# Another seven-product form for probabilities times values in a Conformer block, with four sums a pair, one convolution tap on ScalarE, and five orders moved

## The chip, the cores and the metric

The kernel runs on one core of one Trainium2 chip. A core has TensorE (PE, with a separate row PEld for its weight loads), VectorE (DVE), ScalarE (ACT), GpSimd (POOL) and SyncE (SP); each takes its instructions strictly in the order in which the program issues them, and waits at the head of its queue where an operand is not ready. SP issues nearly all DMAs, so they start in its order too. The metric is the time of one execution on the device in microseconds (us).

## The reference, cut to what matters

One Conformer block in bfloat16, with two sequences of 4000 tokens, D = 512 and F = 2048:

```python
h = _layernorm(x);  x1 = x + 0.5 * (_silu(h @ w_ff1_a) @ w_ff1_b)
h = _layernorm(x1)
p = softmax((h @ w_q) @ (h @ w_k).T * D**-0.5)          # per sequence, 4000 x 4000
x2 = x1 + (p @ (h @ w_v)) @ w_o
h = _layernorm(x2) @ w_pw1                               # 512 -> 1024
h = h[..., :D] * _sigmoid(h[..., D:])
dc = h[t-1] * dw[0] + h[t] * dw[1] + h[t+1] * dw[2]      # depthwise, 3 taps
dc = (dc - mean over all tokens) / sqrt(var + 1e-05)
x3 = x2 + _silu(dc) @ w_pw2
h = _layernorm(x3)
return _layernorm(x3 + 0.5 * (_silu(h @ w_ff2_a) @ w_ff2_b))
```

## The kernel before, in words

**Stages.** Tokens are cut into 16 chunks (eight a sequence) of 508, that is four tiles of 127; the last chunk of each sequence has 444. The stages follow one another: the first feed-forward layer (ff1), attention, and an end with the convolution, pw2 and the second feed-forward layer (ff2). Attention has 16 blocks g of queries, one per chunk, and each has 32 steps kt, one per tile of 128 keys. In the steady state a step is about 2 us and a block about 65.5 us.

**Folded weights.** Queries carry the product of w_q and w_k, so the keys are the normalised rows themselves, and w_v and w_o are folded into one matrix that is applied after the product with the values (`project`). Hence the "values" h[kt] are the normalised rows too: 128 keys by 512, and batch 1's replace batch 0's in block 8.

**Products by seven.** Scores of tile kt go to one of three PSUM banks (a ring, also used by the query groups, the convolution's pw1 and the projection), and ScalarE writes their exponentials to SBUF (`exp_pair`, all ScalarE work has line 710). Two key tiles make a pair; 15 pairs, one tile alone (`P30`) and a tail of 32 keys (`ptail`) make the 4000 keys. A pair by the two halves of the queries, and the 512 columns of the values by their two halves, is a product of 2 x 2 blocks, done with seven block products instead of eight. Each needs sums of probabilities (`pair_sums`, DVE, once a query block, line 1466, over a group of two pairs at a time) and sums of values (`v_sums`, line 1553, once a sequence; `v_here` for batch 0, `v_ahead` and `v_back` for batch 1, through DRAM buffers vhd and vfd). The seven products accumulate over all pairs in PSUM banks 3 to 7 (`PV_BANK`, `pv`, `pv_rest` for the lone tile and the tail), and `pv_join` (line 1527, and copies on ScalarE) combines the banks to the output. Since there are five banks for seven products, two products of a block are computed after others have been joined: `units` issues the work of a block step by step and `units_late` the rest of it in the first steps of the next block; `attention_end` does the latter for the last block. Row sums of probabilities accumulate in `acc` (lines 1472 and 1475), are split into two bfloat16 parts (`split_sums`, lines 1795 and 1796), turned to one column per query by SP's DMA transposes (`sums_by_query`; the issue shows as line 718), and divide the projected rows (`project`, `residual`, line 925).

**What else runs in attention.** `att_hook` adds, per step, the layernorm of the block's chunk before (`ln_job` at kt 9, its tiles' statistics and norms deferred by the numbers of its plan), the transposition of these norms by DMA (line 718, tile `work`), pw1 and the gate of the convolution (`conv_b`, `conv_a`, line 1887), and the three taps with their statistics (`taps_beside`, lines 1917, 1918, 1925, 1928) for chunks whose pw1 is done. `put_x` and `get_x` store and fetch the residual rows.

**What sets the order.** The order is written out by hand. Work that is not issued in place is deferred:

```python
def after(self, n, fn):
    self.later.append((self.tick_n + n, self.seq, fn))
```

and `tick()` at the end of each step issues what is due; `after(n)` called in step kt runs at the end of step kt + n - 1. Semaphore waits are emitted by `Sync.op` from the buffers that an instruction reads and writes. All matmuls have line 660.

**The lines of the change's other places.** ff1 ends with `late`, a table of plans for the layernorms of the last three chunks, which run in the first steps of attention. `keys_swap` places `v_here`, `v_ahead` and `v_back`; `tail_scores` computes the 32-key tail, adds it to the row sums (line 1754) and sends it through DRAM to `ptail`. `wa_back` (line 1073) loads 2 MB of summed ff2 weights (wsd) for ff2; it is issued in ff2's first chunk.

Of the kernel before, what the change touches and what calls it, by code (L numbers as in the profile page):

```python
# [259 lines left out]
class Conformer:  # L260
# [31 lines left out]
    def memory(self):  # L292
# [34 lines left out]
        self.Tt = [E.view(x, self.NTS * HC).rearrange("p (n k) -> p n k", k=HC) for x in (oTe, oTo)]  # L327
        self.b_T = [[E.buf("T", x + n * 2 * HC, 2 * HC) for n in range(self.NTS)] for x in (oTe, oTo)]
# [69 lines left out]
        homes = [(self.XR, 8192 + i * 1536) for i in range(10)] + [(C, oP + i * 1536) for i in range(PAIRS - 10)]  # L398
        self.VF = [Q.view(x, 3 * HD).rearrange("p (m d) -> p m d", m=3) for Q, x in homes]
        self.b_VF = [Q.buf("VF", x, 3 * HD * 2) for Q, x in homes]  # L400

        def both(i):
            Q, x = homes[i]
            n = min(2, PAIRS - i)
            return Q.view(x, n * 3 * HD).rearrange("p (n m d) -> p n m d", n=n, m=3)

        self.VF2 = [both(2 * j) for j in range(FC // 2)]
# [4 lines left out]
        self.vfd = nc.dram_tensor("vfd", [PAIRS, 128, 3 * HD], BF16, kind="Internal").ap()  # L412
        self.b_vhd = [Buf("vhd") for _ in range(PAIRS)]
        self.b_vfd = [[Buf("vfd") for _ in range(2)] for _ in range(PAIRS)]
# [1007 lines left out]
    def next_queries(self, g, kt, at):  # L1422
# [5 lines left out]
        if g + 1 < NCK and kt in ((3, 4, 14, 16) if g == 1 else (14, 16, 18, 20)):  # L1428
            self.q_group((g + 1) // TCB, (g + 1) % TCB, (3, 4, 14, 16).index(kt) if g == 1 else (kt - 14) // 2)
# [6 lines left out]
    def exp_pair(self, g, kt, ps, b_ps):  # L1436
# [5 lines left out]
        lo, hi = ((oR + n * 4 * HC, oTe + m * 2 * HC), (oTo + m * 2 * HC, oR + n * 4 * HC + 2 * HC))[odd]  # L1442
# [3 lines left out]
                 [self.b_R[n] if not odd else self.b_R2[n], self.b_T[odd][m]], scale=SCALE)  # L1446

    def pair_sums(self, g, j, step):
# [168 lines left out]
    def units_late(self, o, kt):  # L1617
# [20 lines left out]
        elif kt < 7:  # L1638
# [8 lines left out]
            if kt == 4:  # L1647
                self.pv_join(o, 5)
# [829 lines left out]
```

## Time and profile before

| | |
|---|---|
| median of 3 runs | 1917.2 us (1916.89 to 1919.14) |
| profiled execution | 1916.96 us, span 1912.9 us from first to last instruction |
| mean granted TensorE clock | 0.999 |
| ff1, 0 to 411 us | PE busy 408.43 us, DVE 336.98, ACT 289.52 |
| attention, 420 to 1435 us | PE 1010.47, DVE 757.25, ACT 431.75 |
| end with ff2, 1435 to 1912 us | PE 469.56, DVE 396.41, ACT 344.48 |

In the profile a group or an instruction is named by its line, its engine, its operation and `out<-in`, the tiles by the program's names: `sums` holds probabilities and their sums, `work`, `wff`, `xt` and `keys` are large regions used for several things, `s` and `y` are PSUM banks (0 to 3 and 4 to 7). SPq is SP's queue as it issues DMAs. A timeline line has the start in us, the length in us, the instruction, how many of a kind follow in one, and in brackets the idle time before it and what ended it. A line of the waits has the engine and tile, the line, the releaser, and then the idle time in all, the number of waits and the longest, in us.

### The profile page before, as it was taken

How to read it: one execution, taken by the hardware profiler on the slowest of the kernel's cores; microseconds unless marked ns; L12 is line 12 of the kernel's file. 1: busy time of each engine (PE TensorE's matmuls, PEld its weight loads, DVE VectorE, ACT ScalarE, POOL GpSimd, SP SyncE). 2: the span in 40 equal slices, each digit the busy share in tenths (PEclk: the TensorE clock that was granted, in tenths of full speed). 3: DMA queues.
4: the chain of work that ended last, by engine and by line, in shares of the span. 5: the costliest groups of instructions: out<-in, count | busy, mean ns of one | idle time of the engine just before them, and what ended most of it. 6: DMA issues, size and time to landing. Idle time of an engine off the chain costs nothing.

```text
span 1912.9 us, 35411 instructions
## 1 busy us (share of the span) xinstructions
PE 1896.8 (99%) x14186; PEld 1400.5 (73%) x14186; DVE 1496.7 (78%) x3220; ACT 1070.2 (56%) x1828; POOL 122.9 (6%) x235
## 2 busy tenths in 40 slices
PE   9999999999999999999999999999999999999998
PEld 6899999966666656666666566566665898999897
DVE  7788888767767787777777776767788888888885
ACT  5677777744443444344434434443447677777774
POOL 1000000000000000000000000000002000000000
PEclk9999999999999999999999999999999999999999
DMA  8233344293223332224821211221146222312211
GB/s 187 72 89 86 81 113 108 70 234 108 77 70 86 85 86 73 53 56 98 202 54 50 55 34 43 56 51 43 40 110 192 76 70 67 76 50 53 64 43 43
DMA packets 284731, 158.04 MB, mean 83 GB/s; under 512 B 204424, under 2 KB 271307, under 8 KB 284303
## 3 DMA queue, kind: packets, MB, share of 16 engines
q1 hardware_dynamic: 283881, 155.37, 32.3%
q8 instruction: 113, 1.85, 0.4%
q14 instruction: 59, 0.48, 0.1%
q10 hardware_dynamic: 678, 0.34, 0.1%
HBM read 62.24 MB, written 48.18 MB: 58 GB/s over the span
## 4 chain that ended last, share of the span: by engine, by line
PE 94%; DVE 3%; DMA 2%; ACT 1%; SPq 1%; issue 0%; POOL 0%; POOLq 0%; DVEq 0%; ACTq 0%
PE s L660 53%; PE y L660 40%; DMA work<-work 1%; DVE work L773 1%; ACT work L710 0%; DMA sums<-in_w_ff_a_dram 0%; DVE xt L925 0%; SPq L718 0%; DMA wff<-in_w_ff_a_dram 0%; DMA wff<-keysd 0%; DVE sums L1466 0%; DMA pqd<-wff 0%; DVE sums L1065 0%; SPq L722 0%; DVE work L958 0%
## 5 line engine op out<-in xcount | busy, mean ns | idle before, releaser
L710 ACT ACTIVATE sums<-s 128x508 bf16<-128x508 f32 (+2 forms) x608 | 355.9, 586 | 473.2 <-PE s L660 455.1
L660 PE MATMUL s<-work,keys 128*128 128x508 bf16 (+3 forms) x2240 | 505.5, 357 | 1.6 <-ACT sums L710 1.1
L660 PEld LDWEIGHTS s<-work,keys 128*128 128x128 bf16 (+1 forms) x2240 | 191.7, 97 | 159.9 <-issue 9.5
L710 ACT ACTIVATE keys<-s 128x508 bf16<-128x508 f32 (+1 forms) x281 | 163.8, 586 | 175.6 <-PE s L660 112.2
L1466 DVE TENSOR_TENSOR sums<-sums 128x508 bf16<-128x508 bf16 (+3 forms) x640 | 218.9, 396 | 35.8 <-ACT sums L710 32.8
L660 PE MATMUL y<-work,keys 128*127 128x256 bf16 x1920 | 244.7, 273 | 0.0
L660 PEld LDWEIGHTS y<-work,keys 128*127 128x127 bf16 x1920 | 216.3, 137 | 5.2
L660 PE MATMUL y<-wff,keys 128*127 128x256 bf16 (+3 forms) x1560 | 209.3, 277 | 0.6 <-DVE xt L1012 0.5
L773 DVE BATCH_NORM_STATS2 work<-xt 127x6 f32<-127x512 bf16 x311 | 199.3, 681 | 2.9 <-DMA xt<-in_x_dram 2.8
L660 PE MATMUL s<-sums 128*128 128x254 bf16 x1296 | 194.4, 273 | 1.6 <-DVE s L1121 1.6
L660 PE MATMUL s<-work,wff 128*128 128x508 bf16 (+4 forms) x884 | 185.5, 352 | 2.6 <-DMA work<-work 2.3
L660 PEld LDWEIGHTS y<-wff,keys 128*127 128x127 bf16 (+1 forms) x1560 | 175.8, 136 | 12.2 <-DVE xt L1012 1.6
L710 ACT ACTIVATE work<-xt,work 127x512 bf16<-127x512 bf16 x204 | 161.6, 808 | 16.9 <-DVE work L785 15.8
L971 DVE TENSOR_TENSOR keys<-keys 128x1016 bf16<-128x1016 bf16 x240 | 160.3, 680 | 2.8 <-ACT keys L710 0.7
L780 POOL TENSOR_TENSOR work<-work 127x4 f32<-127x4 f32 (+1 forms) x76 | 77.2, 1016 | 1153.8 <-DVE work L778 1153.8
L660 PE MATMUL s<-work 128*127 128x512 bf16 (+2 forms) x557 | 142.7, 381 | 1.3 <-DVE work L2091 1.2
L660 PEld LDWEIGHTS s<-sums 128*128 128x128 bf16 x1296 | 126.7, 98 | 19.9 <-DVE s L1121 1.9
L1475 DVE TENSOR_TENSOR work<-work,sums 128x508 f32<-128x508 f32 (+1 forms) x208 | 139.4, 670 | 1.1
L660 PE MATMUL y<-sums,xt 128*128 128x254 bf16 (+1 forms) x960 | 139.1, 269 | 0.8 <-DVE sums L1466 0.8
L660 PEld LDWEIGHTS s<-work,wff 128*128 128x128 bf16 x884 | 81.6, 98 | 75.5 <-issue 3.8
L660 PE MATMUL y<-work,wff 128*128 128x254 bf16 (+1 forms) x892 | 135.3, 274 | 0.0
L660 PEld LDWEIGHTS y<-sums,xt 128*128 128x128 bf16 x960 | 92.9, 97 | 57.6 <-DVE sums L1466 1.3
(151 smaller groups left out, 2510.6 us busy)
## 6 DMA issues: line engine op xcount, KB each, us to landing
xd<-xt SPq DMA_DIRECT2D x28, 448.0 KB, 2.8
xt<-xd SPq DMA_DIRECT2D x28, 448.0 KB, 3.5
out_dram<-xt SPq DMA_DIRECT2D x14, 448.0 KB, 3.2
dcvd<-wff SPq DMA_DIRECT2D x48, 127.0 KB, 2.0
keys<-dcvd SPq DMA_DIRECT2D x12, 508.0 KB, 4.7
xt<-in_x_dram SPq DMA_DIRECT2D x13, 448.0 KB, 4.4
wff<-in_w_ff_b_dram SPq DMA_DIRECT2D x8, 512.0 KB, 7.3
keys<-keysd SPq DMA_DIRECT2D x32, 128.0 KB, 2.9
```

The lines of the kernel that those rows point to most:

```text
L660: self.S.op("PE", lambda e: e.matmul(out, lhsT, rhs, start=start, stop=stop, **kw), reads=reads, writes=[bank], inc=stop if inc is None el ...
L710: return self.S.op("ACT", lambda e: e.activation(out, in_, func, **kw), reads=reads, writes=writes)
L773: self.S.op("DVE", lambda e: e.bn_stats(self.st[sl][:, ti, 0:6], x), reads=[b_x], writes=[self.b_st[sl][ti]])
L780: S.op("POOL", lambda e: e.tensor_tensor(out=self.rs[sl][:, 0:n], in0=self.mv[sl][:, 0:n, 1], in1=self.neghalf[0:TILE, 0:n], op=ALU.pow), ...
L971: self.S.op("DVE", lambda e, out=out, x=x, y=y, op=op: e.tensor_tensor(out=out, in0=x, in1=y, op=op), reads=rd, writes=wr)
L1466: S.op("DVE", lambda e: e.tensor_tensor(out=out, in0=x, in1=y, op=op), reads=rd, writes=wr)
L1475: S.op("DVE", lambda e: e.tensor_tensor(out=acc, in0=acc, in1=sig[step - 5], op=ALU.add), reads=b_f[0:2] + [self.b_acc[s]], writes=[self.b ...
```

## The change

Seven products stay, in another form. With a11, a21 the exponentials of the even key tile for the two query halves and a12, a22 those of the odd one, four sums are formed in a chain, s1 = a21 + a22, s2 = s1 - a11, s3 = a11 - a21 (in a21's place) and s4 = a12 - s2, where there were five. Each exponential instruction now writes both its halves into one kind of buffer. The row sums of the pairs accumulate (s4, s1), and since s4 + s1 = a11 + a12 one addition at the end of the block (the fold) makes them the sums of both halves. The tail is added to the row sums by one instruction over 32 partitions (`sum_tail`) from `ptail`, instead of four. Values' sums are four chained single-width subtractions, and lie in two buffers, V4 and V12; V4 has its own loads in block 8. The joins are two copies on ScalarE and five additions on DVE, instead of three and six. Product 1 now reads raw value tiles and is the first of a block, at step 7; the raw tiles were first read at step 9. The work left for the next block's first steps is in another order (`late_first`, `late_second`, `late_third`).

The multiplication of the first tap is done on ScalarE (Identity with a scale per partition) in place of DVE's tensor_scalar.

Five orders are moved: the layernorm of chunk 14 at the start of attention (plan 2,2,3,3,4,6,6,6,7,7 to 5,5,6,6,7,8,8,9,9,10); batch 0's sums of values (group 0 before attention, group j three steps earlier) and batch 1's (one step later); the layernorm before the convolution one tick earlier; block 1's query groups (3,4,14,16 to 3,4,12,14) and the last block's fetches (15,20,25 to 16,24,31); and the load of the summed ff2 weights, from ff2's first chunk to right behind `attention_end`.

The diff, cut to its core (buffers' declarations, the code of `v_sums` and the old body of `attention_end` are left out):

```diff
-        lo, hi = ((oR + n * 4 * HC, oTe + m * 2 * HC), (oTo + m * 2 * HC, oR + n * 4 * HC + 2 * HC))[odd]
+        lo, hi = ((oTo + m * 2 * HC, oTe + m * 2 * HC), (oR + n * 4 * HC, oR + n * 4 * HC + 2 * HC))[odd]
...
-        a11, a22 = R[:, :, 0], R[:, :, 1]
-        te, to = [t[:, m:m + n, 0:hw] for t in self.Tt]
-        b_te, b_to = [b[m:m + n] for b in self.b_T]
-        b_11, b_22 = self.b_R[r:r + n], self.b_R2[r:r + n]
-        f = [ft[:, k, 0:n, 0:hw] for k in range(3)]
-        if step < 5:
-            out, x, y, op, rd, wr = ((f[0], a11, to, ALU.add, b_11 + b_to, [b_f[0]]),
-                                     (f[1], te, a22, ALU.add, b_te + b_22, [b_f[1]]),
-                                     (f[2], a11, a22, ALU.add, b_11 + b_22, [b_f[2]]),
-                                     (te, te, a11, ALU.subtract, b_te + b_11, b_te),
-                                     (to, to, a22, ALU.subtract, b_to + b_22, b_to))[step]
+        a12, a22 = R[:, :, 0], R[:, :, 1]
+        a11, a21 = [t[:, m:m + n, 0:hw] for t in self.Tt]
+        b_11, b_21 = [b[m:m + n] for b in self.b_T]
+        b_12, b_22 = self.b_R[r:r + n], self.b_R2[r:r + n]
+        s4, s1, s2 = [ft[:, k, 0:n, 0:hw] for k in range(3)]
+        if step < 4:
+            out, x, y, op, rd, wr = ((s1, a21, a22, ALU.add, b_21 + b_22, [b_f[1]]),
+                                     (s2, s1, a11, ALU.subtract, b_11 + [b_f[1]], [b_f[2]]),
+                                     (a21, a11, a21, ALU.subtract, b_11 + b_21, b_21),
+                                     (s4, a12, s2, ALU.subtract, b_12 + [b_f[2]], [b_f[0]]))[step]
             S.op("DVE", lambda e: e.tensor_tensor(out=out, in0=x, in1=y, op=op), reads=rd, writes=wr)
             return
         acc = self.acc[s][:, 0:W].rearrange("p (h k) -> p h k", h=2)
+        if step == 6:
+            S.op("DVE", lambda e: e.tensor_tensor(out=acc[:, 0], in0=acc[:, 0], in1=acc[:, 1], op=ALU.add),
+                 reads=[self.b_acc[s]], writes=[self.b_acc[s]])
+            return
         sig = [ft[:, 0:2, k, 0:hw] for k in range(n)]
         if j == 0:
-            if step == 5:
+            if step == 4:
                 S.op("DVE", lambda e: e.tensor_tensor(out=acc, in0=sig[0], in1=sig[1], op=ALU.add),
                      reads=b_f[0:2], writes=[self.b_acc[s]])
-        elif step - 5 < n:
-            S.op("DVE", lambda e: e.tensor_tensor(out=acc, in0=acc, in1=sig[step - 5], op=ALU.add),
+        elif step - 4 < n:
+            S.op("DVE", lambda e: e.tensor_tensor(out=acc, in0=acc, in1=sig[step - 4], op=ALU.add),
                  reads=b_f[0:2] + [self.b_acc[s]], writes=[self.b_acc[s]])
 
-    PV_BANK = {1: 4, 6: 5, 7: 6, 5: 7, 3: 7, 2: 3, 4: 3}
+    PV_BANK = {1: 4, 6: 5, 7: 6, 5: 7, 3: 3, 2: 4, 4: 6}
 
...
-            form, b_1, mv, b_2 = {1: (v[:, 0], b_v, f[:, 2], b_f[2]), 2: (he[:, 0:HD], b_he, f[:, 1], b_f[1]),
-                                  3: (he[:, HD:D], b_he, R[:, 0], self.b_R[r]), 4: (ho[:, 0:HD], b_ho, R[:, 1], self.b_R2[r]),
-                                  5: (ho[:, HD:D], b_ho, f[:, 0], b_f[0]), 6: (v[:, 1], b_v, T[0], self.b_T[0][m]),
-                                  7: (v[:, 2], b_v, T[1], self.b_T[1][m])}[n]
+            he, ho, v4, v12 = self.h[2 * i], self.h[2 * i + 1], self.V4[i // 2][:, i % 2], self.V12[i // 2][:, i % 2]
+            b_he, b_ho, b_v4, b_v12 = self.b_h[2 * i], self.b_h[2 * i + 1], self.b_V4[i], self.b_V12[i]
+            form, b_1, mv, b_2 = {1: (he[:, 0:HD], b_he, T[0], self.b_T[0][m]), 2: (ho[:, 0:HD], b_ho, R[:, 0], self.b_R[r]),
+                                  3: (ho[:, HD:D], b_ho, f[:, 0], b_f[0]), 4: (v4[:, 0], b_v4, R[:, 1], self.b_R2[r]),
+                                  5: (v12[:, 0], b_v12, f[:, 1], b_f[1]), 6: (v12[:, 1], b_v12, f[:, 2], b_f[2]),
+                                  7: (he[:, HD:D], b_he, T[1], self.b_T[1][m])}[n]
...
-        forms = {5: (v[:, HD:D], b_v, 0), 2: (v[:, 0:HD], b_v, 1), 7: (vs, b_vs, 0), 6: (vs, b_vs, 1)}
+        forms = {3: (v[:, HD:D], b_v, 0), 7: (v[:, HD:D], b_v, 1), 2: (v[:, 0:HD], b_v, 0), 4: (vs, b_vs, 1)}
...
         if step == 0:
-            self.act(t2, y(2)[0][:, 0:W], AF.Copy, [y(2)[1]], [b_t2])
+            self.act(t2, y(1)[0][:, 0:W], AF.Copy, [y(1)[1]], [b_t2])
         elif step == 1:
-            dve(t2, 5, t2, b_t2, ALU.add, [b_t2])
+            dve(t2, 6, t2, b_t2, [b_t2])
         elif step == 2:
-            dve(t2, 1, t2, b_t2, ALU.subtract, [b_t2])
-        elif step < 5:
-            out, b_out = rr[step - 3]
-            dve(out, (7, 6)[step - 3], t2, b_t2, ALU.add, [b_out])
+            dve(u4, 5, t2, b_t2, [b_u4])
+        elif step == 3:
+            dve(half(1, 2), 7, u4, b_u4, self.b_OTq[1][2:4])
+        elif step == 4:
+            dve(half(0, 2), 3, u4, b_u4, self.b_OTq[0][2:4])
+        elif step == 5:
+            dve(half(1, 0), 4, t2, b_t2, self.b_OTq[1][0:2])
         else:
-            k = step - 5
-            ps, b_ps = y((2, 5)[k])
-            self.act(half(1 - k, 2 * k), two(ps[:, 0:W]), AF.Copy, [b_ps], self.b_OTq[1 - k][2 * k:2 * k + 2])
-            dve(half(k, 2 * k), (2, 5)[k], *rr[k], ALU.add, self.b_OTq[k][2 * k:2 * k + 2])
+            self.act(half(0, 0), two(y(2)[0][:, 0:W]), AF.Copy, [y(2)[1]], self.b_OTq[0][0:2])
...
+    def late_first(self, o):
+
+        end = PAIRS // 2 - 1
+        for n in (1, 6):
+            self.pv(o, n, self.group(end))
+            self.pv(o, n, self.group(end + 1))
+        self.pv_join(o, 0)
+        self.pair_sums(o, end + 1, 4)
+        self.pair_sums(o, end + 1, 6)
+        self.sum_plain(o, KT - 2, self.P30, self.b_P30)
+        self.sum_tail(o)
+        self.pv_join(o, 1)
+
+    def late_second(self, o):
+
+        end = PAIRS // 2 - 1
+        self.pv(o, 5, self.group(end + 1))
+        self.pv_join(o, 2)
+        self.pv(o, 7, self.group(end))
+        self.pv(o, 7, self.group(end + 1))
+        self.pv(o, 3, self.group(end + 1))
+        for tail in range(2):
+            self.pv_rest(o, tail, (7, 3, 2))
+        self.pv_join(o, 3)
+        self.pv_join(o, 4)
+
+    def late_third(self, o, n, pairs):
+
+        self.pv(o, n, pairs)
+        if pairs and pairs[-1] == PAIRS - 1:
+            if n == 4:
+                for tail in range(2):
+                    self.pv_rest(o, tail, (n,))
+            self.pv_join(o, 6 if n == 2 else 5)
+
     def units_late(self, o, kt):
 
-        end, last = PAIRS // 2 - 1, o == NCK - 1
         if kt == 0:
-            self.pv(o, 1, self.group(end))
-            self.pv_rest(o, 0, (2, 5))
-            self.pv(o, 2, self.group(end + 1))
-            self.pv(o, 5, self.group(end + 1))
-            self.pv_rest(o, 1, (2, 5))
-            self.pv_join(o, 0)
-            self.pair_sums(o, end + 1, 5)
-            self.sum_plain(o, KT - 2, self.P30, self.b_P30)
+            self.late_first(o)
         elif kt == 1:
-            for n in (6, 7):
-                self.pv(o, n, self.group(end))
-            for n in (1, 6, 7):
-                self.pv(o, n, self.group(end + 1))
-            self.pv_rest(o, 0, (7, 6))
-            self.pv_rest(o, 1, (7, 6))
-            self.pv_join(o, 1)
-            self.pv_join(o, 2)
+            self.late_second(o)
         elif kt < 7:
             m = (kt - 2) * 6
-            for n in range(m, m + 6):
-                self.pv(o, 3 if n >= PAIRS else 4, [n % PAIRS])
+            self.late_third(o, 2, range(m, min(m + 6, PAIRS)))
+            self.late_third(o, 4, range(max(m - PAIRS, 0), max(m + 6 - PAIRS, 0)))
             if kt == 2:
                 self.split_sums(o)
                 self.sums_by_query(o % TCB % 2, 5)
-                self.pv_join(o, 3)
-                self.pv_join(o, 4)
-            if kt == 4:
-                self.pv_join(o, 5)
-            if kt == 6:
-                self.pv_join(o, 6)
...
-            order = ((1, 6), (7,), (2,), (5,)) if j == 0 else ((2, 5), (1,), (6,), (7,))
+            order = ((1, 6), (5,), (3,), (7,)) if j == 0 else ((5, 3), (1,), (6,), (7,))
             for n in order[r]:
                 self.pv(g, n, self.group(j))
         j, r = divmod(kt - 4, 4)
         if 0 <= j <= end:
-            for n in ((0, 1), (2, 3, 4), (5,), (6,))[r]:
+            for n in ((0, 1), (2, 3), (4,), (5,))[r]:
...
+        o = NCK - 1
+        self.late_first(o)
         self.act(self.nr1, self.onef, AF.Sigmoid, [self.b_onef], [self.b_nr1])
-        self.pair_sums(o, end + 1, 5)
-        self.sum_plain(o, KT - 2, self.P30, self.b_P30)
         self.split_sums(o)
         self.tick()
+        self.late_second(o)
+        self.sums_by_query(o % TCB % 2, 6)
         self.tick()
-        self.pv(o, 4, range(PAIRS))
-        self.pv_join(o, 5)
+        self.late_third(o, 2, range(PAIRS))
         self.tick()
-        self.pv(o, 3, range(PAIRS))
-        self.pv_join(o, 6)
+        self.late_third(o, 4, range(PAIRS))
...
-            j, r = divmod(kt - 3, 3)
-            if 0 <= j <= G and r < 2:
+            j, r = divmod(kt, 3)
+            if 0 < j <= G and r < 2:
...
-            for n in {0: (0,), 3: (1, 2), 4: (3, 4), 7: (5,)}.get(r, ()):
+            for n in {0: (0,), 4: (1, 2), 5: (3, 4), 8: (5,)}.get(r, ()):
...
-                    self.v_back(j, True)
+                    self.v_back(j, 1)
                 if at == KT + 5 + j:
-                    self.v_back(j, False)
+                    self.v_back(j, 0)
+                if at == KT + 13 + j:
+                    self.v_back(j, 2)
...
+    def sum_tail(self, g):
+        S, s, W = self.S, g % TCB % 2, width(g)
+        acc = self.acc[s][0:REST, 0:W]
+        S.op("DVE", lambda e: e.tensor_tensor(out=acc, in0=acc, in1=self.ptail[0:REST, 0:W], op=ALU.add),
+             reads=[self.b_ptail, self.b_acc[s]], writes=[self.b_acc[s]])
...
-        S.op("DVE", lambda e: e.tensor_scalar(tmp, g[:, 0:W], w[0], None, ALU.mult), reads=rd, writes=[b_tmp])
+        self.act(tmp, g[:, 0:W], AF.Identity, rd, [b_tmp], scale=w[0])
...
-                late = (self.SOON, (2, 2, 3, 3, 4, 6, 6, 6, 7, 7), (18, 18, 19, 19, 20, 22, 22, 23, 24, 25))
+                late = (self.SOON, (5, 5, 6, 6, 7, 8, 8, 9, 9, 10), (18, 18, 19, 19, 20, 22, 22, 23, 24, 25))
...
+        if not any_score:
+            for n in range(4):
+                self.v_here(0, n)
...
-                self.ln_job(g - 1, "in", "ACT", (2, 3, 4, 5, 6, 7, 8, 8, 9, 9), slot=0)
+                self.ln_job(g - 1, "in", "ACT", (1, 2, 3, 4, 5, 6, 7, 7, 8, 8), slot=0)
...
-                if kt in (15, 20, 25):
-                    self.get_x(kt // 5 - 3, self.slot(kt // 5 - 3, 2))
+                if kt in (16, 24, 31):
+                    self.get_x(kt // 8 - 2 + kt // 31, self.slot(kt // 8 - 2 + kt // 31, 2))
...
             self.attention_end()
+        self.wa_back()
...
-                if c == 0 and f == 3:
-                    self.wa_back()
```

More of the change, by code (lines that the diff above doesn't have):

```diff
@@ L1445, in exp_pair @@
         self.act(out, ps[:, 0:W].rearrange("p (h k) -> p h k", h=2), AF.Exp, [b_ps],
-                 [self.b_R[n] if not odd else self.b_R2[n], self.b_T[odd][m]], scale=SCALE)
+                 [self.b_R[n], self.b_R2[n]] if odd else [self.b_T[0][m], self.b_T[1][m]], scale=SCALE)
     def pair_sums(self, g, j, step):
@@ L1546, in v_sums @@
     def v_sums(self, x, f1, f2, b_x, b_1, b_2, step):
[L1548 to L1553 removed]
+        t4, t1, t2 = f1, f2[:, :, 0], f2[:, :, 1]
@@ L1558, in v_here @@
-        self.v_sums(self.hp[j], f[:, :, 0], f[:, :, 1:3], self.b_h[4 * j:4 * j + 2 * n], b_f, b_f, step)
+        self.v_sums(self.hp[j], self.V4[j][:, :, 0], self.V12[j], self.b_h[4 * j:4 * j + 2 * n], self.b_V4[2 * j:2 * j + n],
+                    self.b_V12[2 * j:2 * j + n], step)
     def v_rest(self, k):
         x = self.h[KT - 2 + k]
-        self.S.op("DVE", lambda e: e.tensor_tensor(out=self.Vs[k], in0=x[:, 0:HD], in1=x[:, HD:D], op=ALU.add),
+        self.S.op("DVE", lambda e: e.tensor_tensor(out=self.Vs[k], in0=x[:, 0:HD], in1=x[:, HD:D], op=ALU.subtract),
```

90 lines of the change are left out of this document (32 added, 58 removed).

## Prediction

> **What bounds the kernel now.** I read the busy shares first, then the waits of TensorE (PE), then the timeline at each wait.
>
> ```profile
> PE 1896.8 (99%) x14186; PEld 1400.5 (73%) x14186; DVE 1496.7 (78%) x3220; ACT 1070.2 (56%) x1828; POOL 122.9 (6%) x235
> 420.00:1435.00 1015.00, 1010.47 (x6798) 631.09 (x6798) 757.25 (x1696) 431.75 (x742) 46.71 (x126) 1.00 0.30 74
> ```
>
> PE is busy 99% of the span. The second line is attention, where the change sits (PE, weight load, DVE, ACT, POOL): PE 1010.47 of 1015 us, DVE 757, ACT 432. The matmul work is the same after the change (below), so the time can only move where PE waits:
>
> ```profile
> PE s L660 <- DMA work<-work: 2.3, 3, 0.9
> PE s L660 <- DVE s L1121: 1.6, 2, 1.2
> PE s L660 <- ACT sums L710: 1.1, 2, 0.7
> ```
>
> These (sum, number, longest) and smaller ones make about 9 us that an order could recover. Where they lie (start, length, idle before):
>
> ```profile
> 420.23 1.05 PE L660 MATMUL y<-sums,xt 128*128 128x254 bf16 x8 [0.84 <-DVE sums L1466]
> 579.96 0.29 DVE L1553 TENSOR_TENSOR work<-wff 128x256 bf16<-128x256 bf16 x1 [2.31 <-DMA wff<-keysd]
> 589.55 0.39 PE L660 MATMUL s<-sums,keys 128*128 128x254 bf16 x2 [0.43 <-DVE sums L1466]
> 896.39 1.89 PE L660 MATMUL s<-work,wff 128*128 128x508 bf16 x8 [0.59 <-DMA work<-work]
> 960.23 1.69 PE L660 MATMUL s<-work,wff 128*128 128x381 bf16 x16 [0.77 <-DMA work<-work]
> 1466.38 4.33 SPq L1073 DMA_DIRECT2D sums<-wsd  x2
> 1492.39 0.61 PE L660 MATMUL s<-sums 128*128 128x254 bf16 x4 [1.20 <-DVE s L1121]
> ```
>
> I count a loss as the time from one matmul's start to the next, less its columns at 0.417 ns: it is somewhat above the wait printed.
>
> **The change part by part**, against the profiled execution: 1916.96 us, span 1912.9 with 4.06 around it; the median of the runs, 1917.2, is 0.24 above.
>
> *Probability sums, row sums, joins.* Products stay seven per pair, 15 pairs, two matmuls each; single tile and tail keep their matmuls and their four switches a block between 128- and 32-row matmuls. PE: 0. DVE loses 8 of 40 sums a block, 16 x 8 x 396 ns (row L1466) = 51 us at most; the four 32-row adds (L1754, 282 ns each) become one; added are a fold (half the columns of row L1475's 670 ns, so about 0.4 us) and a tail add (0.6, the same row); one join fewer, 686 ns (L1527). All this ran while PE was 99.6% busy, so it counts 0; its cover is PE's scores and products, and without it DVE's 757 us would still be below 1010.
>
> Joins: the last join was an ACT copy and a DVE add, after the last product; now it is one DVE add. PE waited 0.25 at 1435.14: -0.25. Bounds: 0, if the residual chain behind it ends last; -0.8, the copy's 0.6 whole and the wait.
>
> *Product 1 takes raw value tiles.* In block 8 these come back from DRAM, and are now needed at step 7, not step 9.
>
> ```profile
> 916.83 3.01 SPq L718 DMA_TRANSPOSE work<-work  x2
> 924.69 0.43 SPq L714 DMA_DIRECT2D keys<-vhd  x1
> 928.39 1.03 PE L660 MATMUL y<-sums,xt 128*128 128x254 bf16 x8
> ```
>
> SP works without a pause from 916.83 to the load at 924.69, which landed 3.42 us later, 928.11: 0.28 ahead of the matmul that now wants it. The transposes at 916.83 wait for the split of the row sums (L1796), which now stands behind the fold and the tail add, 0.4 + 0.6 us, and one more join in DVE's order, 0.7: landing about 929.5. PE takes its work in order, so the scores of step 8 and exp(8) stand behind this matmul and the whole wait counts. I take +1.3; bounds 0 (DVE's four fewer sums bring the split forward) and +2.5 (two joins ahead of it). The eight extra loads, of 128 KB like others at 2.9 us, follow on SP at steps 13 to 20 and are needed in the first steps of block 9: 0.
>
> *Sums of batch 1's values (v_ahead) one step later.* DVE stood 2.31 us at 579.96 for a DMA, and PE then lost 0.33 at 583.74 and 0.60 at 589.55. One step is about 1.65 us; the wait shrinks to 0.66 and everything behind it on DVE comes earlier: -0.93, between -0.93 and 0 (another sum is late then). Elsewhere DVE stands shorter with no wait of PE behind it: 0. Batch 0's sums (v_here) move from steps 3 on to before attention: four DVE operations of some 0.29 to 0.42 us, in the start below.
>
> *Norm before the convolution, one tick earlier.* Its transposes fed the three late matmuls at 896.39, 960.23, 1411.94 (lost 0.75, 0.93, 1.07). In block 7 the second pair was issued 892.36 to 894.86; a tick (2 us) and the earlier norms bring it some 4 us forward: -0.75. In block 8 likewise: -0.93. In block 15 SP ran four transposes back to back, 5.12 us from 1404.37, and the norm's store (0.85 us of issue) and a load (0.9) now stand between: earlier and later cancel: 0, between -1.07 and +1.0. In blocks 1 to 6 and 9 to 14 no wait is there. Sum -1.68. Queries of block 1 go two steps earlier (POOL and SP idle there): 0. The loads of block 15 at 16, 24, 31 instead of 15, 20, 25 leave the residual at 1392.28, which cost 0.47, a freer DVE: -0.4 (0 to -0.47).
>
> *First tap on ScalarE.*
>
> ```profile
> L1917 DVE TENSOR_SCALAR wff<-wff,work 128x508 f32<-128x508 bf16 x49 | 23.4, 478 | 0.0
> L710 ACT ACTIVATE work<-keys,work 128x508 bf16<-128x508 bf16 x56 | 44.4, 801 | 0.2 <-DVE work L2003 0.2
> L710 ACT ACTIVATE keys<-sums 128x508 bf16<-128x508 f32 x108 | 66.7, 618 | 3.6 <-DVE sums L1121 3.3
> 1080.77 1.51 ACT L710 ACTIVATE work<-xt,work 127x512 bf16<-127x512 bf16 x2
> 1082.18 0.58 ACT L710 ACTIVATE sums<-s 128x508 bf16<-128x508 f32 x1
> 1082.65 1.51 ACT L710 ACTIVATE work<-xt,work 127x512 bf16<-127x512 bf16 x2
> 1083.53 1.02 PE L660 MATMUL s<-work,keys 128*128 128x508 bf16 x4
> ```
>
> DVE saves 478 ns a tap. ACT has none with one pointer: between 618 (none) and 801 (two), 0.7 taken. It falls in two steps of each block. At step 16 (block 10 shown) four norms of 0.75 precede exp(17), which ended at 1082.76, and PE wants its bank at 1083.53: slack 0.77 against 0.70 to 0.80. I take +0.2 in all (0 to 12 blocks x 0.3 = +3.6). At step 28 product 3 of group 6 has 1.8 us of slack, 0.5 afterwards: 0.
>
> [...]
>
> *Attention start.*
>
> ```profile
> 419.93 1.52 ACT L710 ACTIVATE work<-xt,work 127x512 bf16<-127x512 bf16 x2 [2.50 <-DVE work L785]
> 421.98 1.03 PE L660 MATMUL s<-work,keys 128*128 128x508 bf16 x4 [0.71 <-ACT sums L710]
> ```
>
> PE lost 2.46 here: 1.01 at 420.23, where DVE's sums were late, 0.87 and 0.58 at 421.98 and 423.87, where exp stood behind the norms that waited for DVE. The value sums of group 0, now done earlier, free DVE: -1.0. But chunk 14's statistics are asked for three steps later and its norms two, so I place their shift at about 423.1; the first norm now stands between exp(6), which leaves ACT free at about 419.2, and exp(7), which ends at 424.5, after PE wants its bank: about 2.0 at step 10 and 0.6 at step 11, 2.6 in all. So +0.15, between -2.46 (the norm falls clear) and +2.0 (two steps wait).
>
> *Load of the summed ff2 weights (wsd) moved to the end of attention.* Its 2 MB, landing 11.8 us after issue, slowed the transposes that DVE stood 2.15 us for until 1483.92, and PE lost 1.36 at 1492.39. SP idles 1430 to 1440, ahead of the last store and Wp2's load, needed at 1462: -1.25 (0 to -1.36).
>
> Sum: -0.25 + 1.3 - 0.93 - 1.68 - 0.4 + 0.2 + 0.15 - 1.25 = -2.86. 1916.96 - 2.86 = 1914.1; on the scale of the median 1914.3 us.
>
> **The rivals.** (1) *The start falls clear and the block 8 load lands in time.* SP's 0.28 us margin and DVE's freedom speak for it; the norms of chunk 14 on ACT against. 1914.3 - 0.15 - 2.46 - 1.3 - 0.2 = 1910.2.
> (2) *The waits re-form.* Sums, statistics, joins and taps share DVE's one queue and the transposes, stores and loads SP's, so what goes earlier in one place is paid for by the next in line: in the 2.31 us at 579.96, DVE's sums ahead are as late as before if the load is. Against it: DVE and SP stand idle for a quarter of attention and more. Nothing moves: 1917.2.
> (3) *The multiply on ScalarE holds exp(17) in every block with taps* (3 to 14). It decides when the norms, the tap and the exponential end after PE reaches scores 19: slack 0.77 by one block. If the norm, tap and exponential queue in another order, the whole 0.7 is lost: 12 x 0.7 = 8.4, so 1914.3 - 0.2 + 8.4 = 1922.5. Against: 0.77 exceeds 0.70.
>
> **How the numbers follow.** Measured runs differ by up to 0.12%, so 0.2% (3.8 us: 1913.4 and 1921.0) is about what can be told from no change. Forecast 0.42 (1911.9 to 1916.5, 0.17 of it below 1913.4); rival 1, 0.18; rival 2, 0.15; rival 3, 0.25, of which 0.04 below 1921. Faster 0.17 + 0.18 = 0.35; same 0.25 + 0.15 + 0.04 = 0.44; slower 0.21. All bounds together give 1908.2 to 1926.1; 8 in 10 is 1909.6 to 1922.5, the upper end rival 3 whole.
>
> **What would show it.** No wait of PE for the DMA at the pairs of blocks 7 and 8; none at 583 to 590 and 1492; a wait for keys<-vhd of about 1.3 at the start of block 8; at each step 16 a PE wait for ACT below 0.1 (0.7 under rival 3); the ACT row of the tap near 0.7 us; L1466 with 512 operations. Wrong if PE waits for the sums of the last group (steps 30 and 31), whose products 1 and 6 stand first in the next block, with about 0.5 us to spare by the trace.

## The result and the profile after

The changed kernel takes 1931.19 us (median of 5 runs, 1927.62 to 1934.7) against 1917.35 us for the kernel before beside it: a ratio of 1.007, 95% interval 1.0053 to 1.0086. It is slower by some 14 us, and above the whole range that was given. The profiled execution is the slowest of the five, 1934.7 us with a span of 1930.3.

The busy shares on the page, and the window of attention, which now ends near 1452 us instead of 1435 (PE, weight load, DVE, ACT, POOL, granted clock, DMA share, GB/s):

```profile
PE 1901.7 (99%) x14183; PEld 1401.9 (73%) x14186; DVE 1434.3 (74%) x2991; ACT 1091.4 (57%) x1865; POOL 129.5 (7%) x235
420.00:1452.00 1032.00, 1014.57 (x6794) 632.12 (x6792) 695.60 (x1470) 452.64 (x777) 54.63 (x127) 0.99 0.30 74
```

DVE lost 62 us of busy time, 25 of them the tap's multiplications, and the time did not follow. PE's own work is the same but for 4 us more of busy time in attention, and that comes with a clock of 0.99 where it was 1.00. So the time is in waits, and in that clock. The longest of PE's waits in the changed kernel (engine, tile, line, releaser; sum, number, longest):

```profile
PE s L658 <- ACT work L708: 7.6, 1, 7.6
PE s L658 <- DMA work<-work: 2.8, 1, 2.8
PE y L658 <- DMA keys<-vhd: 2.5, 1, 2.5
PE s L658 <- ACT sums L708: 2.2, 2, 1.7
```

The first three are single waits, new or grown, 12.9 us in all. Most lines of the new kernel have moved by a few: 658 is the matmul, 708 ScalarE, 1463 the sums.

*The first, 445 us, in block 0.* The timeline, with SP's issues:

```profile
433.78 0.43 SPq L712 DMA_DIRECT2D wff<-in_w_pw_dram  x1
435.93 2.39 SPq L904 DMA_DIRECT2D keysd<-work  x2
444.48 0.59 ACT L708 ACTIVATE work<-s 128x508 bf16<-128x508 f32 x1 [10.69 <-DMA keysd<-work]
445.13 1.88 PE L658 MATMUL s<-work 128*128 128x508 bf16 x4 [7.64 <-ACT work L708]
```

The third line is ScalarE's eviction of a query group, into a part of `work` that held chunk 14's normalised keys until their store to DRAM had landed. In the kernel before, the store was issued here, and nobody waited for it:

```profile
429.26 0.97 SPq L906 DMA_DIRECT2D keysd<-work  x2
```

The later norms moved its issue by 6.7 us, behind 16 loads of 128 KB, of which seven had stood ahead of it, and behind the 1 MB load of w_pw1. Its last piece landed 8.5 us after the issue. ScalarE stood 10.7 us at the head of its queue, with the exponentials behind it, and PE 7.6.

*The second, 940.6, at the start of block 8; the third, 1427.8, in block 15:*

```profile
936.11 0.43 SPq L712 DMA_DIRECT2D keys<-vhd  x1
940.59 1.03 PE L658 MATMUL y<-sums,keys 128*128 128x254 bf16 x4 [2.51 <-DMA keys<-vhd]
...
1416.02 2.50 SPq L716 DMA_TRANSPOSE work<-work  x2
1418.56 1.05 SPq L597 DMA_DIRECT2D xd<-xt  x2
1419.66 1.38 SPq L608 DMA_DIRECT2D xt<-xd  x2
1421.08 2.50 SPq L716 DMA_TRANSPOSE work<-work  x2
1427.78 2.75 PE L658 MATMUL s<-work,wff 128*128 128x508 bf16 x8 [2.84 <-DMA work<-work]
```

In block 15 the store and one fetch of residual rows, each in two pieces, now stand between the two pairs of transposes. The second pair ends its issue at 1423.58, and PE gets its rows 4.2 us later; before, the four were issued one behind the other and PE had the rows 2.45 us after the end of the issue (1409.49 to 1411.94):

```profile
1404.37 5.12 SPq L718 DMA_TRANSPOSE work<-work  x4
1411.94 1.24 PE L660 MATMUL s<-work,wff 128*128 128x508 bf16 x5 [0.91 <-DMA work<-work]
```

*Behind each of the three waits PE runs at half clock for a while.* The windows right behind the three, and, first, one around a shorter gap (1.9 us, at the start of attention) that had no such thing behind it; the granted clock is the third number from the end:

```profile
425.00:428.00 3.00, 1.66 (x9) 0.81 (x10) 1.78 (x5) 3.00 (x6) 0.00 (x0) 1.00 0.63 126
445.10:448.90 3.80, 3.77 (x10) 1.48 (x11) 3.20 (x8) 1.70 (x4) 0.00 (x0) 0.50 0.02 4
940.50:944.40 3.90, 3.81 (x17) 2.18 (x18) 1.31 (x3) 0.25 (x1) 0.00 (x0) 0.56 1.18 282
1427.70:1431.80 4.10, 4.02 (x12) 1.61 (x13) 1.15 (x2) 0.59 (x1) 0.41 (x1) 0.61 0.38 73
```

Matmuls of 508 columns start 0.42 us apart there instead of 0.21. By starts of matmuls less their columns the three places lost 7.81 + 1.88, 2.67 + 1.67 and 3.00 + 1.67 us (gap and half clock), 18.7 in all; the kernel before had lost 1.07 at the last and nothing at the others. The span grew by 17.4.

### The profile page after: what moved, and what is told of

Same layout as the page of the kernel before. It is cut to its first block, busy times and chain, and to the rows that moved or that the text cites. A ratio compares the mean times of both kernels' runs of the same rounds, so it can differ in the third digit from the quotient of the medians.

```text
span 1930.3 us, 35274 instructions
## 1 busy us (share of the span) xinstructions
PE 1901.7 (99%) x14183; PEld 1401.9 (73%) x14186; DVE 1434.3 (74%) x2991; ACT 1091.4 (57%) x1865; POOL 129.5 (7%) x235
## 4 chain that ended last, share of the span: by engine, by line
PE 94%; DVE 2%; DMA 1%; SPq 1%; ACT 0%; issue 0%; POOL 0%; POOLq 0%; DVEq 0%
PE s L658 51%; PE y L658 43%; DVE work L771 1%; SPq L712 0%; DMA sums<-in_w_ff_a_dram 0%; DMA keysd<-work 0%; SPq L716 0%; DMA work<-work 0%; DMA wff<-in_w_ff_a_dram 0%; DMA keys<-vhd 0%; ACT work L708 0%; DVE xt L923 0%; DVE sums L1063 0%; SPq L720 0%; SPq L904 0%
## 5 line engine op out<-in xcount | busy, mean ns | idle before, releaser
L708 ACT ACTIVATE sums<-s 128x508 bf16<-128x508 f32 (+2 forms) x592 | 344.5, 585 | 464.6 <-PE s L658 462.1
L1463 DVE TENSOR_TENSOR sums<-sums 128x508 bf16<-128x508 bf16 (+3 forms) x512 | 190.2, 397 | 31.3 <-ACT sums L708 23.2
L658 PE MATMUL y<-sums,keys 128*128 128x254 bf16 (+1 forms) x1440 | 198.3, 270 | 2.5 <-DMA keys<-vhd 2.5
L658 PEld LDWEIGHTS y<-sums,keys 128*128 128x128 bf16 x1440 | 139.4, 97 | 69.5 <-DMA keys<-vhd 3.0
L778 POOL TENSOR_TENSOR work<-work 127x4 f32<-127x4 f32 (+1 forms) x76 | 81.8, 1077 | 1154.2 <-DVE work L776 1154.2
```

The lines of the kernel that those rows point to most:

```text
L658: self.S.op("PE", lambda e: e.matmul(out, lhsT, rhs, start=start, stop=stop, **kw), reads=reads, writes=[bank], inc=stop if inc is None el ...
L708: return self.S.op("ACT", lambda e: e.activation(out, in_, func, **kw), reads=reads, writes=writes)
L778: S.op("POOL", lambda e: e.tensor_tensor(out=self.rs[sl][:, 0:n], in0=self.mv[sl][:, 0:n, 1], in1=self.neghalf[0:TILE, 0:n], op=ALU.pow), ...
L1463: S.op("DVE", lambda e: e.tensor_tensor(out=out, in0=x, in1=y, op=op), reads=rd, writes=wr)
```

## The experiments

**One part undone at a time.** Four kernels are the changed one with one edit each. Chunk 14's plan as before:

```diff
-late = (self.SOON, (5, 5, 6, 6, 7, 8, 8, 9, 9, 10), ...
+late = (self.SOON, (2, 2, 3, 3, 4, 6, 6, 6, 7, 7), ...
```

> The changed kernel with one order undone: chunk 14's layernorm plan at the start of attention is 2,2,3,3,4,6,6,6,7,7 again. Theory: the loss at 445 us is made by the store of chunk 14's keys (keysd<-work), which the later norms put behind 16 loads and the 1 MB load of w_pw1 on SP (issued 435.93, landed about 444.4); ACT's eviction of the query group waits for it, PE stands 7.8 us and then runs at half clock, 9.7 us in all. With the plan back the store is issued near 429, the wait and the half clock go: 6 to 10 us less than the changed kernel's 1931.2, so about 1921 to 1925. Rival: the store stays late because SP's queue is full of the value loads anyway: 1931 within 2 us.

Measured: 1920.42 us, 10.8 below the changed kernel, at the ratio 1.0017 (1.0007 to 1.0026) to the kernel before. The store is issued at 429.32 again, and PE's wait for ScalarE's eviction is down from 7.6 to 0.6:

```profile
PE s L658 <- DMA work<-work: 2.9, 1, 2.9
PE y L658 <- DMA keys<-vhd: 2.6, 1, 2.6
...
PE s L658 <- ACT work L708: 0.6, 1, 0.6
```

The theory holds for this place; the gain is a little above the 6 to 10 us that were expected. The same order alone, put into the kernel before:

```diff
-late = (self.SOON, (2, 2, 3, 3, 4, 6, 6, 6, 7, 7), ...
+late = (self.SOON, (5, 5, 6, 6, 7, 8, 8, 9, 9, 10), ...
```

> The kernel before with one order of the change alone: chunk 14's layernorm plan 5,5,6,6,7,8,8,9,9,10. Theory (the order alone makes the store late, whatever the form of the product): a wait of ACT for keysd<-work near 440 us, PE standing 5 to 8 us and half clock behind it, 7 to 11 us slower than before, 1924 to 1928. Rival (it needs the denser queue of the changed kernel too): within 3 us of 1917.

Measured: 1925.96 us, ratio 1.0047 (1.0031 to 1.0062). One table of ten numbers costs 8.7 us by itself, with the old product and the tap on DVE. In its trace ScalarE waits for the store and PE for ScalarE:

```profile
442.72 0.59 ACT L710 ACTIVATE work<-s 128x508 bf16<-128x508 f32 x1 [8.76 <-DMA keysd<-work]
443.37 1.88 PE L660 MATMUL s<-work 128*128 128x508 bf16 x4 [5.72 <-ACT work L710]
```

Was the store late because it was issued late, or because the 1 MB went ahead of it? The changed kernel with that load at another step:

```diff
-if g == 0 and kt == 8:
+if g == 0 and kt == 18:
     self.load(self.Wp1, ...
```

> The changed kernel with chunk 14's plan as changed, but the 1 MB load of w_pw1 in block 0 issued at step 18 instead of step 8, so that it no longer goes ahead of the store of chunk 14's keys. Theory A (the store is slow because its 448 KB share the DMA engines with the 1 MB just ahead): the store lands some 4 to 5 us earlier, the stall at 445 us shrinks from 7.8 to about 3, 1924 to 1927. Theory B (the store is late because it is issued late, behind 16 other loads): the issue moves by 0.5 us only and the stall stays at about 7, 1930 to 1931.

Measured: 1925.86 us, 5.3 below the changed kernel. In its trace:

```profile
433.83 0.97 SPq L904 DMA_DIRECT2D keysd<-work  x2
436.00 0.81 SPq L712 DMA_DIRECT2D wff<-in_w_pw_dram  x1
439.05 0.59 ACT L708 ACTIVATE work<-s 128x508 bf16<-128x508 f32 x1 [6.57 <-DMA keysd<-work]
439.70 1.87 PE L658 MATMUL s<-work 128*128 128x508 bf16 x4 [3.53 <-ACT work L708]
```

Without the 1 MB ahead the store took 5.2 us instead of 8.5 and went out 2.1 us sooner (theory B had 0.5); PE's wait halved, and the time is as theory A had it. But the transfer is not the whole: the store still goes out 4.6 us later than in the kernel before, and PE still waits 3.5 us. About half of the wait is the transfer ahead, half the place in SP's queue.

Product 1 of a block's first group at step 9:

```diff
-order = ((1, 6), (5,), (3,), (7,)) if j == 0 ...
+order = ((6,), (5,), (1, 3), (7,)) if j == 0 ...
```

> The changed kernel with product 1 of the first group of each block at step 9 instead of step 7, so that raw value tiles are first read at step 9 as before the change. Theory: PE's 2.5 us wait for keys<-vhd at 940.6 and the half clock behind it (4.3 us in all) go, and nothing else moves: about 1927, 4 us below 1931.2. Rival: the load is late by more than two steps, or the wait goes to the next product: a wait for keys<-vhd of over 1 us stays, and the time is within 1.5 us of 1931.

Measured: 1928.14 us, 3.0 less where 4 were expected. The wait for keys<-vhd is gone from the list and came back nowhere in that block.

The old plan of the convolution's norm in block 15 alone:

```diff
-self.ln_job(g - 1, "in", "ACT", (1, 2, 3, 4, 5, 6, 7, 7, 8, 8), slot=0)
+self.ln_job(g - 1, "in", "ACT", (1, 2, 3, 4, 5, 6, 7, 7, 8, 8) if g < NCK - 1 else (2, 3, 4, 5, 6, 7, 8, 8, 9, 9), slot=0)
```

> The changed kernel with the plan of the layernorm before the convolution as of old (2,3,4,5,6,7,8,8,9,9) in block 15 alone. Theory: there the store and the fetches of residual rows got between the two pairs of transposes, so that the second pair landed at 1427.8 and PE waited 2.8 us and then ran at half clock, 4.7 us with the 0.7 ahead of it, against 1.07 before; with the store ahead of all norms the four transposes go together: 3 to 4 us less than 1931.2, about 1927.5. Rival: the transposes are late because the value sums and taps make the norms late in this block: the wait stays above 2 us and the time within 1.5 us of 1931.

Measured: 1927.14 us, 4.0 less, and the wait is that of the kernel before:

```profile
PE s L658 <- DMA work<-work: 0.9, 1, 0.9
```

**Together, and what is left.** The three edits (chunk 14's plan, step 9, block 15) in one kernel:

> The changed kernel with the three single edits together: chunk 14's plan as before, product 1 of the first group at step 9, the old plan of the convolution's norm in block 15 alone. Theory (three late DMAs make the whole loss and are independent): 1931.2 less the three measured gains of 10.8 to 14 together with 3.0 and 4.0 is 1913 to 1914, 3 us below the kernel before; waits of PE for keys<-vhd and for keysd<-work gone, for work<-work about 0.9. Rival (the waits re-form elsewhere, or the sums and the tap cost time of their own): 1917 or more.

Measured: 1917.92 us, ratio 1.0002 (0.9993 to 1.0011): level with the kernel before, and 4.6 us short of the sum of the single gains. The rival was right in part: waits re-formed. One place is seen in the trace:

```profile
PE s L658 <- ACT sums L708: 2.1, 1, 2.1
...
PE y L658 <- DVE work L1527: 1.2, 1, 1.2
```

The first line is at the start of attention. Product 1 at step 9 in every block leaves PE less to do in block 0 while the norms hold the exponential; the gap there grew from 1.79 us (in the kernel with the plan alone undone, which differs in block 0 by step 9 only) to 2.22, and half clock followed, 1.7 us. The last line is the end of attention, where the product whose bank is joined on DVE waits for that join. In the changed kernel it is at 1449 us:

```profile
1446.14 0.53 DVE L1797 CAST work<-work 128x381 bf16<-128x381 f32 x1
1446.71 0.56 DVE L1798 TENSOR_TENSOR work<-work 128x381 bf16<-128x381 f32 x1
...
1448.32 0.62 DVE L1527 TENSOR_TENSOR work<-y,work 128x444 bf16<-128x444 f32 x1
...
1449.00 2.17 PE L658 MATMUL y<-sums,work 128*128 128x222 bf16 x21 [1.16 <-DVE work L1527]
```

The split of the row sums stands ahead of the joins. With it behind them, on top of the three edits:

```diff
-self.split_sums(o)
 self.tick()
 self.late_second(o)
+self.split_sums(o)
```

> As the kernel with the three edits, and in attention_end the split of the row sums into two parts (lines 1797 and 1798) is put behind the late products and joins of the second step instead of ahead of them. Theory: PE's new wait of 1.2 us for the join (1449.0 in the changed kernel) comes from the four split operations ahead of the joins on DVE, 1.6 us; it goes and the time is 1.0 to 1.3 us less than with the three edits alone. Rival: the row sums then come late to the projection behind it and PE waits there: no difference.

Measured: 1916.25 us, 1.7 less than the kernel with three edits. The wait for L1527 is gone. And with the tap on DVE besides:

```diff
-self.act(tmp, g[:, 0:W], AF.Identity, rd, [b_tmp], scale=w[0])
+S.op("DVE", lambda e: e.tensor_scalar(tmp, g[:, 0:W], w[0], None, ALU.mult), reads=rd, writes=[b_tmp])
```

> As the kernel before it in this list (three edits and the split moved), with the first tap's multiplication on DVE again. Theory: the tap costs nothing on either engine, within 1 us of that kernel. Rival (the tap on ScalarE holds the exponential in the blocks with taps): up to 8 us less with the tap on DVE. Other rival (the tap on ScalarE is what lets the sums of the first blocks be in time): 1 to 2 us more.

Measured: 1913.85 us, 2.4 less again, ratio 0.998 (0.9972 to 0.9989). "The tap costs nothing" was wrong. The tap alone, undone in the changed kernel:

> The changed kernel with the first tap's multiplication on DVE again and nothing else undone. Theory (the second tap on DVE waits at the head of its queue for ScalarE's first, 114 us in the changed kernel, and sums of probabilities queue behind it): PE's waits for L1463 at 1383 and 1420 us (0.7 and 0.7) go, 1.5 to 3 us less than 1931.2. Rival (the 2.4 us seen between the two kernels with three edits were chance of the half clock): within 1 us of 1931.2.

Measured: 1926.82 us, 4.4 less than the changed kernel and more than was expected (five runs of each, 1924.3 to 1929.38 here). What it does is seen in the changed kernel's groups, ScalarE's first tap, and DVE's second, with the idle time ahead of it in the last column:

```profile
L708 ACT ACTIVATE wff<-wff,work 128x508 f32<-128x508 bf16 x49 | 34.7, 709 | 0.0
L1920 DVE SCALAR_TENSOR_TENSOR wff<-wff,work 128x508 f32<-128x508 bf16 x49 | 36.6, 747 | 105.1 <-ACT wff L708 105.1
```

The price on ScalarE is as forecast, 709 ns. But the second tap on DVE needs it, and stands 2.15 us on the mean at the head of DVE's queue, behind the exponentials, and in part the norms, that ScalarE has to do first; everything behind it on DVE is late. With the tap on DVE, PE's waits for L1463 at 1383 and 1420 us are gone. At block 8 the split of the row sums comes 0.87 us earlier against PE's tail matmuls, and the wait for keys<-vhd falls from 2.5 to 0.7, with no half clock:

```profile
PE y L658 <- DMA keys<-vhd: 0.7, 1, 0.7
```

The load itself also took 1.0 us less from its issue to PE's start there (3.5 against 4.5); what it collided with in the changed kernel was not settled. In block 15 this trace has a longer wait instead, 3.9 us for the transposed rows where it was 2.8, so the gain is net of that.

**The product by itself**: the first tap on DVE and all orders as before, but for the last block's fetches, which can't go back since the values' sums now lie under them.

```diff
 the edits to the tap and chunk 14's plan as above, in all blocks the old plan of the norm,
 v_here at 3 + 3 j, v_ahead {0, 3, 4, 7}, block 1's query groups (3, 4, 14, 16), wa_back in ff2's first chunk
```

> The changed kernel with the first tap on DVE and the orders as before (chunk 14's plan, both value sums, the convolution's norm, the query groups, the load of wsd), so that only the product with four sums, its joins and its late order are left, and the last block's fetches, which stay where the change put them, since the new home of the values' sums lies under them. Theory: the product itself costs PE only its wait for keys<-vhd in block 8 with the half clock behind it, 3.0 to 4.3 us, and the join at the end, 1.2: about 1921 to 1922 against 1917. Rival: the chain of four sums delays PE in every block: over 1925. Other rival: the freed DVE gains what the orders need: at most 1918.

Measured: 1918.37 us, ratio 1.0006 (0.9998 to 1.0015). Not the 1921 to 1922 of the theory: the wait for keys<-vhd is 0.6 instead of 2.5 and has no half clock behind it. The product is level with the old one by this measurement. It takes DVE's work away, and DVE was not the bound.

**The half clock by itself.** The kernel before, with ScalarE held back by copies of a scratch tile at steps 10 and 20 of blocks 4 to 14:

```diff
+if 4 <= g < NCK - 1 and kt in (10, 20):
+    n = 2 * (g - 4) + kt // 20
+    for w in [CHUNK] * (3 + n // 2) + [CHUNK // 2] * (n % 2):
+        self.act(self.tmp[:, 0:w], self.tmp[:, 0:w], AF.Copy, [self.b_tmp], [self.b_tmp])
 if kt < KT - 2:
     self.exp_pair(g, kt, ps, b_ps)
```

> The kernel before with ScalarE held back on purpose at steps 10 and 20 of blocks 4 to 14 by copies in place of a scratch tile, 1.8 us in all at the first place and 0.3 us more at each next one, so that PE meets 22 gaps of growing length. It measures the half clock by itself. Theory (what counts is how much of a fixed stretch of some 3 to 3.5 us PE stands still): no half clock after gaps below 1.6 us, always after gaps above 3.4, either way between these, and each time 1.4 to 1.9 us are lost whatever the gap. Rival (a gap must be longer than a fixed length): one length separates the gaps with half clock from those without. Other rival (the half clock comes from the DMAs running then, not from PE's gap): no half clock after any gap here.

It ran once, 2000.45 us; what counts is its trace. Gap of PE and time lost to half clock behind it, worked out from the starts of its matmuls, in us:

```
gap   1.07  1.13  1.47  2.13  2.35  2.43  2.79  3.00  3.44  3.66  4.10  4.31  4.76  4.97  5.42  5.63  6.39
lost  0     0     0     0     1.60  1.54  1.70  1.66  1.33  1.61  1.68  1.12  2.37  1.64  2.55  2.74  2.60
```

In the other kernels' traces gaps of 1.75, 2.22 (three times), 2.58 and 2.67 us had it behind them, and gaps of 1.65, 1.79, 1.90, 2.73 and 3.10 had not. So no single length parts them; up to 1.65 us none had it, from 3.44 us on all. That the loss is 1.4 to 1.9 whatever the gap was wrong as well: it is 1.12 to 2.74 here.

The granted clock shows more. In the changed kernel's trace half clock begins at 442.18, 940.53 and 1428.63 us and lasts 6.83, 3.41 and 3.41 us; the starts are 498.35 and 488.10 us apart, 146 and 143 times 3.413. Three pairs of windows of the kernel with the copies, cut in such steps from the starts of half clock in its own trace, each with the gap in the first and what followed in the second (the second number is PE's busy time):

```profile
897.06:900.47 3.41, 1.12 (x22) 0.53 (x21) 0.00 (x0) 3.31 (x8) 0.00 (x0) 1.00 0.72 162
900.47:903.88 3.41, 3.41 (x12) 1.52 (x11) 1.69 (x5) 0.76 (x3) 0.00 (x0) 0.50 0.64 189
1013.11:1016.52 3.41, 1.45 (x10) 1.02 (x10) 1.02 (x3) 2.36 (x5) 0.00 (x0) 1.00 0.01 2
1016.52:1019.94 3.42, 3.42 (x22) 2.06 (x21) 2.77 (x6) 0.59 (x1) 0.00 (x0) 1.00 0.02 5
1238.39:1241.80 3.41, 1.35 (x9) 0.96 (x9) 0.23 (x1) 2.42 (x5) 0.00 (x0) 1.00 0.02 5
1241.80:1245.22 3.42, 3.42 (x13) 1.76 (x11) 1.71 (x3) 0.59 (x1) 0.00 (x0) 0.50 0.00 0
```

They hold the gaps of 2.35, 2.13 and 4.10 us. In the third pair half clock followed with next to no DMAs (5 and 0 GB/s), so the other rival, the DMAs, fell. The gap of 3.10 us, in the kernel with step 9, fell on two windows, left PE busy for half of the second, and had no half clock behind it:

```profile
1417.55:1420.96 3.41, 2.18 (x30) 1.20 (x27) 3.21 (x8) 1.35 (x3) 0.00 (x0) 1.00 1.66 95
1420.96:1424.37 3.41, 1.71 (x8) 0.81 (x9) 0.00 (x0) 0.59 (x1) 0.00 (x0) 1.00 0.40 93
1424.37:1427.79 3.42, 3.42 (x26) 2.31 (x25) 1.99 (x4) 1.49 (x3) 0.63 (x2) 1.00 0.57 152
```

Cut so from 22 to 1917 us, the changed kernel's own trace has three windows at full clock in which PE was busy for less than 1 us (0.00 from 438.77, 0.97 from 937.11, 0.85 from 1425.22), and half clock followed each; the next has 2.1 us, and none followed it or any with more. In the windows above it followed 1.12 and 1.35 us of PE's work and not 1.45 or 1.71. These agree with the theory of a fixed stretch; a rule for it was not shown, nor one for the loss.

**A version that beats both.** Product 1 at step 9 in block 8 alone, the old plans for chunk 14 and block 15, the split behind the joins, the tap on DVE, batch 0's sums of values at their old steps; the new product, v_ahead, the earlier norm in the other blocks and the new place of wsd stay.

```diff
-order = ((1, 6), (5,), (3,), (7,)) if j == 0 else ...
+order = ((6,), (5,), (1, 3), (7,)) if j == 0 and g == TCB else ((1, 6), (5,), (3,), (7,)) if j == 0 else ...
```

> The changed kernel with: chunk 14's plan as before; product 1 of the first group at step 9 in block 8 alone; the old plan of the convolution's norm in block 15 alone; the split of the row sums behind the joins at the end of attention; the first tap on DVE; and batch 0's sums of values at their old steps. Against the kernel with three edits, the split moved and the tap on DVE (1913.85) it differs in the start of attention alone, where that one lost 4.4 us in its trace, 1.6 of them at half clock. Theory: with product 1 at step 7 in block 0 and the value sums as of old the start loses 2.4 as in the trace with the product alone, and no half clock follows: 1911.5 to 1912.5. Rival: the start's loss is set by the norms of chunk 14 on ScalarE, whatever the products do: within 0.7 us of 1913.85.

Measured: 1912.74 us (1911.95 to 1913.39), ratio 0.9977 (0.9967 to 0.9986) to the kernel before. It is 1.1 below the one with step 9 in all blocks, a little less than expected; the start lost 2.4 in its trace, with no half clock. The two differ in batch 0's sums of values too, and which of the two edits gave the 1.1 was not separated.

## Why the prediction was wrong, point by point

*Attention start, the step that failed.* The forecast of the norms was right to a tenth: gaps of 1.90 and 0.58 us against the 2.0 and 0.6 forecast, 2.48 in all where 2.6 was said. But the step ended with the norms. Chunk 14's job also stores its keys, and that store was not priced: neither its place on SP, behind 16 loads and 1 MB, nor who writes next into the rows that it reads. It cost 9.7 us in the trace and 8.7 alone in the kernel before, on a term that was given as +0.15 with +2.0 at most.

*Product 1 on raw tiles.* The mechanism was right, and forecast at +1.3 (0 to 2.5): the gap was 2.67. With the product alone it was 0.81. What the working lacked was the tap's part in it, and the half clock, 1.67 more.

*Norm one tick earlier.* Blocks 7 and 8 went as forecast: 0.6 and 0.9 us less, 1.5 where 1.68 was said. Block 15 was put at 0 with +1.0 at most; it went from 1.07 to 3.00 and 1.67 of half clock. The step counted the store's and the fetch's issue, 1.75 us, as cancelled by the earlier norms; the norms were not early enough to go ahead of them, so the second pair of transposes was issued behind both, and its data came 4.2 us after the issue.

*The tap on ScalarE.* The 0.7 us and the free bank at step 16 were right: PE waits for no exponential there, so rival 3's mechanism fell. Its side was right for another reason. The step asked only what waits on ScalarE behind the tap, not what waits on DVE for it; the saving of 478 ns there became a wait of 2.15 us. It is worth 2.4 us to have it back with the other edits, 4.4 in the changed kernel.

*Last join.* Put at -0.25. The join itself is shorter; but DVE's four split operations now stand ahead of the joins of the second step and PE waits 1.2 us for one of them. Moving them gained 1.7 us.

*v_ahead* gave 0.73 to 0.93 us in the traces, as forecast. *The load of wsd* was put at -1.25: the 1.36 us at 1492 are gone, but a wait of the same kind of 0.7 us stands a little later (1510 in the changed kernel), so it gave about 0.6; rival 2 was right there. *The residual at 1392* is gone (-0.47), and a wait of 0.7 us for sums at 1383 came in, which went with the tap.

*What no term had* is the half clock: 5.2 us of the three places together. Even the bounds all at their worst, 1926.1, stopped short of 1931.

## What to carry to other kernels

Of a job that is moved, follow its last instruction: here the store at its end kept a buffer busy until it had landed, 8.5 us after its issue, and the next writer of that memory was on another engine, ScalarE, which stood 10.7 us with everything of its own behind it. Of an operation that is given to another engine, ask who consumes it: the tap's 709 ns on ScalarE became a wait of 2.15 us on the mean at the head of DVE's queue, paid by all that followed there. And in these runs gaps of PE up to 1.65 us cost only themselves, while some from 1.75 us on, and all from 3.44 us on, cost 1.12 to 2.74 us more; so one long gap cost more there than the same time in short ones.

## What the runs showed of the hardware

The half clock behind a gap was not expected. In these runs it followed some gaps from 1.75 us on and every one from 3.44 us on, with a granted clock of 0.50, and cost 1.12 to 2.74 us in the kernel with the copies; between, like gaps went both ways. The gap of 2.67 us in the changed kernel left PE busy for 0.97 us of one window of 3.41 us, and half clock followed; the gap of 3.10 in the kernel with step 9 fell on two, with 2.18 and 1.71 us, and none followed. Single gains then did not add up: the three edits together stayed 4.6 us short of the sum of their gains, and 1.7 us of that was half clock behind a gap of 2.22 us at the start of attention.

A second point: 448 KB and 60 KB of keys took 8.5 us from issue to their last landing with 1 MB just ahead on the same queue, 5.2 without. How far the transfer ahead and how far the loads before it make this was not separated further.
